# The last 64 rows of a 320-deep product: four half-height products at one place, in the two halves of the rows, in an mLSTM, mixture-of-experts and gated layer kernel

## The chip, the cores and the metric

The kernel runs on one core of a Trainium2 chip. The metric is the device time of one execution in microseconds (us). The kernel before takes 647.97 us (median of three runs, 647.9 to 648.02). TensorE is called PE in the profile and its loading of weights PEld, VectorE is DVE, ScalarE is ACT, GpSimd is POOL, and SyncE (SP) issues the transfers.

## The reference

Three layers follow each other, on 1536 tokens of 320 features.

```python
# 1: mLSTM, 2 batches x 8 heads x 768 steps x 40 features
C = f_stab * C + i_stab * outer(v, k);  n = f_stab * n + i_stab * k
y[t] = sigmoid(o) * (C @ q) / max(|n . q|, 1)
# 2: four experts, D = 320, F = 1024
for e in range(4):
    h = np.maximum(x @ w1[e], 0.0)
    out += p[:, e:e + 1] * (h @ w2[e])
# 3: gated layer, D = 320, F = 1536
return (a * b) @ w_out          # a = x @ w_a, b = x @ w_b
```

All of it is float32. The kernel multiplies in a reduced 32-bit type (`F32R`) and keeps the precision by splitting each operand into a high part and a low part: x = xh + xl, w = wh + wl. A product then is wh·xh + wl·xh + wh·xl; the product of the two low parts is dropped.

## The kernel before, in words

**Blocks.** The weights of layers 2 and 3 are cut into 14 blocks: blocks 0 to 7 for the experts (half an expert, four slices of 128 hidden features each) and blocks 8 to 13 for the gated layer (two slices of 128 hidden features each, with w_a and w_b). Phase one runs layer 1 and, beside it, blocks 0 to 2 on 256 tokens at a time. Phase two runs blocks 3 to 13, each over three chunks `c` of 512 tokens. The two phases are one program on one queue per engine, in the order in which the code records them.

**An item.** An `Item` is one slice `f` of one block on one chunk. Its method `a()` makes the hidden values: one sum (blocks below 8, tile `psa`) or two (blocks 8 and up, `psb` and `psa`) of 128 hidden features by 512 tokens in one of four banks of PSUM that are used in turn; ACT and DVE then make the high part `hh` and the low part `hl` from the sum. Its method `b()` multiplies these by the second weight: 12 products of 320 columns into `psy` (4 groups of 128 tokens, three products each). `Stream.push` calls `a()` of the new item and then `b()` of the item pushed two before it, so TensorE's order is a(f), b(f-2), a(f+1), b(f-1) and so on.

**A sum.** The contraction of 320 is 128 + 128 + 64 rows. `mm_group` makes a sum of eight products of 512 columns and 128 rows each:

```python
(k(wh, 0), x(xh, 0)), (k(wh, 1), x(xh, 1)), (k(wl, 0), x(xh, 0)), (k(wl, 1), x(xh, 1)),
(k(wh, 0), x(xl, 0)), (k(wh, 1), x(xl, 1)), (k(wh, 2), x(xh, 2)), (k(wl, 2), x(xh, 2)),
```

In the third part the 64 rows stand twice: rows 0 to 63 of `xh[c][:, 2]` hold the high part of x and rows 64 to 127 its low part, and the weights stand twice too. So the seventh product gives wh·xh and wh·xl of the last 64 features at once. The eighth gives wl·xh in its upper half; what its lower half adds, low times low, is not needed.

**The split of x.** `split_hi` (ACT) and `split_lo` (DVE) make `xh` and `xl` from the transposed activations in PSUM (`pt_x`, for each of the 12 tiles `n` of 128 tokens): ACT casts all 384 columns to `xh`, DVE makes `xl` (256 columns), and DVE then overwrites rows 64 to 127 of the third part with the low part. This runs 12 times in phase one (`s3b`, and written out for n = 0 and 1) and 12 times around blocks 7 and 8 (`finish_x2`), where the input of layer 3 replaces that of layer 2; there `pt_x2` takes the same four banks of PSUM as the sums, in turn.

**Weights.** The pieces of the blocks are loaded by SP and split by ACT and by DVE or POOL (`piece1`, `piece2`). `Paced` records a stage of them twice an item.

Of the kernel before, what the change touches and what calls it, by code (L numbers as in the profile page):

```python
# [7 lines left out]
F32 = mybir.dt.float32  # L8
F32R = mybir.dt.float32r
BF16 = mybir.dt.bfloat16  # L10
# [3 lines left out]
AF = mybir.ActivationFunctionType  # L14
ALU = mybir.AluOpType
# [3 lines left out]
P = 128  # L19
# [6 lines left out]
NB1, NB2 = 8, 6  # L26
WF1 = 3 * P + DM
WF2 = 6 * P + DM
# [3 lines left out]
NF = 2  # L32
NP = 4
LOENG = {0: "ppvpvpvp", 1: "pppppppp", 2: "pppppppp", 3: "vpvpvpvp", 4: "vpvpvpvp", 5: "vpvpvpvp"}
RB = 3
QB = 3
QENG = ("vector", "vector")
WARM = 10
AHEAD = 2
PACE = ((0, 1.5), (32, 2.4), (62, 2.5))  # L40
NEG = -1.0e30
LOGMIN = -104.0
SQMIN = (1.0625 * 2.0 ** -15) ** 2
# [3 lines left out]
def mlstm_moe_kernel(ctx, tc, gates, qk, qc, kvo, dp, w1b, w2b, ident_d, bdmask_d, rsel_d, exp_d, out):  # L47
    nc = tc.nc
# [3 lines left out]
    wp0 = ctx.enter_context(tc.tile_pool(name="wp0", bufs=3))  # L52
    rawp = ctx.enter_context(tc.tile_pool(name="rawp", bufs=RB))
    xp = ctx.enter_context(tc.tile_pool(name="xp", bufs=1))
# [7 lines left out]

    xh = [xp.tile([P, 3, 512], F32R, name=f"xh{c}") for c in range(3)]
    xl = [xp.tile([P, 2, 512], F32R, name=f"xl{c}") for c in range(3)]
    sums = xp.tile([P, NT * DM], F32, name="acc")
    acc = [sums[:, n * DM:(n + 1) * DM] for n in range(NT)]


    wblk = {}
# [54 lines left out]
    def split_x(ps, c, o):  # L124

        split_hi(ps, c, o)
        split_lo(ps, c, o)
# [3 lines left out]

    def split_lo(ps, c, o):
        nc.vector.tensor_tensor(xl[c][:, :, o:o + P], ps[:, 0:2, :], xh[c][:, 0:2, o:o + P].bitcast(F32), op=ALU.subtract)
        r = xh[c][64:128, 2, o:o + P]
        nc.vector.tensor_tensor(r, ps[64:128, 2, :], r.bitcast(F32), op=ALU.subtract)

# [56 lines left out]
    def mm_group(ps, wh, wl, o0, c, o, n):  # L193
        k = lambda w, t: w[:, o0 + t * P:o0 + (t + 1) * P]
        x = lambda t, i: t[c][:, i, o:o + n]
        prs = [
            (k(wh, 0), x(xh, 0)), (k(wh, 1), x(xh, 1)), (k(wl, 0), x(xh, 0)), (k(wl, 1), x(xh, 1)),
            (k(wh, 0), x(xl, 0)), (k(wh, 1), x(xl, 1)), (k(wh, 2), x(xh, 2)), (k(wl, 2), x(xh, 2)),
        ]
        for i, (l, r) in enumerate(prs):  # L200
            nc.tensor.matmul(ps, l, r, start=(i == 0), stop=(i == len(prs) - 1))  # L201

    class Item:


# [3 lines left out]
        def a(self):  # L209
            blk, f, c, o, n = self.blk, self.f, self.c, self.o, self.n  # L210
            pa, ph = self.pools["a"], self.pools["h"]
            wh, wl = wblk[blk]
            self.hh = ph.tile([P, n], F32R, tag="hh", name="hh")
            self.hl = ph.tile([P, n], F32R, tag="hl", name="hl")
            if blk < NB1:
                ps = pa.tile([P, 512], F32, tag="a", name="psa")[:, :n]
                mm_group(ps, wh, wl, f * WF1, c, o, n)
                nc.scalar.activation(self.hh, ps, AF.Relu)  # L218
                nc.vector.scalar_tensor_tensor(self.hl, ps, 0.0, self.hh.bitcast(F32), op0=ALU.max, op1=ALU.subtract)  # L219
            else:  # L220
                pb = pa.tile([P, 512], F32, tag="a", name="psb")[:, :n]
                mm_group(pb, wh, wl, f * WF2 + 384, c, o, n)
                bs = ph.tile([P, n], F32, tag="bs", name="bs", bufs=2)
                nc.scalar.copy(bs, pb)  # L224
                ps = pa.tile([P, 512], F32, tag="a", name="psa")[:, :n]
                mm_group(ps, wh, wl, f * WF2, c, o, n)
                g = ph.tile([P, n], F32, tag="g", name="g", bufs=2)
                nc.vector.tensor_tensor(g, ps, bs, op=ALU.mult)  # L228
                nc.scalar.copy(self.hh, g)  # L229
                nc.vector.tensor_tensor(self.hl, g, self.hh.bitcast(F32), op=ALU.subtract)  # L230

        def b(self):
            blk, f, fi, nf, n = self.blk, self.f, self.fi, self.nf, self.n
            wh, wl = wblk[blk]
            off = f * WF1 + 384 if blk < NB1 else f * WF2 + 768
            if fi == 0:
                last = (blk, self.c) == (NB1 + NB2 - 1, 2)
                self.pools["bt"] = [self.pools[q].tile([P, DM], F32, tag=q, name="psy") for q in ("aabb" if last else "bbbb")[:n // P]]
            for t in range(n // P):
                ps = self.pools["bt"][t]  # L240
                lh, ll = self.hh[:, t * P:(t + 1) * P], self.hl[:, t * P:(t + 1) * P]
                nc.tensor.matmul(ps, lh, wh[:, off:off + DM], start=(fi == 0), stop=False)  # L242
                nc.tensor.matmul(ps, lh, wl[:, off:off + DM], start=False, stop=False)  # L243
                nc.tensor.matmul(ps, ll, wh[:, off:off + DM], start=False, stop=(fi == nf - 1))  # L244
                if fi == nf - 1:
                    self.done(self.blk, self.c * 4 + self.o // P + t, ps)

    def add_expert(blk, n, ps):
        e = blk // 2
        if blk <= 1:  # L250
            nc.scalar.activation(acc[n], ps, AF.Copy, scale=pg[:, n, 0:1])  # L251
        else:
            nc.vector.scalar_tensor_tensor(acc[n], ps, pg[:, n, e:e + 1], acc[n], op0=ALU.mult, op1=ALU.add)


    stream = Stream(AHEAD)
# [4 lines left out]
    with ExitStack() as c1:  # L261
        cq = ExitStack()
        qp = cq.enter_context(tc.tile_pool(name="qp", bufs=2, side="right"))
        ac = c1.enter_context(tc.tile_pool(name="ac", bufs=1))
# [66 lines left out]
        def gate1(j, eng):  # L331
            mr = a2.tile([G, P + 1], F32, tag="mr", name="mr")
            if j == 0:
                nc.gpsimd.memset(mr[:, 0:1], NEG)
            else:
# [174 lines left out]


        ctx.enter_context(tc.manual_schedule())
        wz = ac.tile([P, 512], BF16, name="wz")
        nc.gpsimd.memset(wz, 0.0)

        def warm_up(n):
# [89 lines left out]
        go(w0[3:4])  # L606
        s2b(1)
        split_lo(td[0]["pv"], 0, 0)
        go(w0[2:4])
        go(w0[4:5])  # L610
        warm_up(4)
        s3a(1)
        split_hi(td[1]["pv"], 0, P)
        split_lo(td[1]["pv"], 0, P)
        warm_up(1)
        go(w0[4:5])
# [18 lines left out]
        for j in range(2, NCH):  # L635
            n0, n1, t0 = 2 * j, 2 * j + 1, NI * (j - 1)
            new = [
                (-6.4, load_kvo, n0), (-6.2, load_o, j, nc.sync), (-2.0, load_kvo, n1),
                (-4.4, load_qk, n0, 0), (-3.4, load_qk, n0, 1), (-2.4, load_qk, n1, 0), (-1.4, load_qk, n1, 1),
                (-4.0, table, AF.Sigmoid), (-3.5, o_gate, j), (-2.5, table, AF.Exp),  # L640
                (-1.5, split_qk, n0, 0), (-0.5, split_qk, n0, 1),
                (0.5, s1a, n0, 0), (1.5, s1a, n0, 1), (1.6, split_qk, n1, 0),
                (2.4, s1b, n0, 0), (2.6, split_qk, n1, 1),
                (3.4, s1b, n0, 1), (3.5, s1a, n1, 0), (3.6, weigh_k, n0),
                (4.2, s2a, n0, 0), (4.5, s2a, n0, 1), (4.6, weigh_k, n1), (4.95, s2b, n0),
# [23 lines left out]
        pools = {"a": ps_a, "b": ps_b, "h": hp}  # L669
# [6 lines left out]
        for k in range(NI * NCH):  # L676
            until(k)
            j, i = k // NI, k % NI
            fi, nf = (i, 8) if i < 8 else (i - 8, 4)
# [10 lines left out]
    pools = {"a": Turns(ps_a2, ps_a), "b": Turns(ps_b2, ps_b), "h": hp2}  # L690
    todo, twice = [], {}

    def finish_x2(n):
        pt = pools["a"].tile([P, 512], F32, tag="a", name="pt_x2")
        pv = pt[:, 0:384].rearrange("p (k t) -> p k t", t=P)
        transpose_x(acc[n], twice[n], pv)
        split_x(pv, n // 4, (n % 4) * P)
# [18 lines left out]
    pieces = [piece1(i, s, slot[i], nc.vector if LOENG.get(i, ())[s:s + 1] == "v" else nc.gpsimd, True) for i in range(4, NB1) for s in range(NP1)]  # L716
    pieces += [piece2(i, s, slot[i]) for i in range(NB1, NB1 + NB2) for s in range(NP2)]
    paced = Paced(pieces, PACE)
    for blk in range(3, NB1 + NB2):
        nf = 4 if blk < NB1 else 2  # L720
        for c in range(3):
            for f in range(nf):
                ready = list(todo)

                def finish(k):
                    for n in ready[:k]:
                        ready.remove(n)
                        todo.remove(n)
                        finish_x2(n)

                def between():
                    paced.step()
                    if blk == NB1:
                        finish(2)

                stream.push(Item(blk, f, f, nf, c, 0, 512, pools, done2), between)
                paced.step()
                finish(2)
    stream.flush()
# [102 lines left out]
```

## Time and profile before

| | |
|---|---|
| median of three runs | 647.97 us |
| the profiled execution, by the clock of the runs | 647.9 us |
| its span in the trace | 646.2 us |
| PE busy | 626.6 us, 97% of the span |
| DVE busy | 419.9 us, 65% |
| ACT busy | 267.2 us, 41% |
| POOL busy | 182.6 us, 28% |
| share of PE in the chain that ended last | 90% |

The span runs from the first to the last instruction of the trace; 1.7 us of the profiled execution lie outside it. Phase one ends at about 221 us. The chain that ended last is followed back from the last instruction, at each step to what released it. A matmul's record is longer than the time that it takes from the next one, since matmuls are pipelined: the distance between starts tells what one costs.

### The profile page before, as it was taken

What the parts mean: (1) busy time and instruction counts of PE and PEld (TensorE: products, weight loads), DVE (VectorE), ACT (ScalarE), POOL (GpSimd) and SP (SyncE); (2) the same over time, 40 slices, a digit from 0 to 9 for tenths busy, and PEclk for the clock granted to TensorE, in tenths of its full rate; (3) what the DMA queues carried; (4) which work ended last, traced back from release to release, by engine and by line L of the source; (5) the groups of instructions that cost most, each with busy time, mean ns of one, the idle gap of its engine ahead of it and who ended that gap; (6) DMA issues with size and microseconds to landing.
All of it is one profiled execution on the core that took longest, in us unless ns stands there. A gap on an engine that the chain in (4) does not pass through costs nothing.

```text
span 646.2 us, 10283 instructions
## 1 busy us (share of the span) xinstructions
PE 626.6 (97%) x3798; PEld 568.6 (88%) x3799; DVE 419.9 (65%) x860; ACT 267.2 (41%) x592; POOL 182.6 (28%) x217
## 2 busy tenths in 40 slices
PE   8887999999999999999999999999999999999997
PEld 6787989999999999999888988888888888888886
DVE  8986858576654244323587888888766776764343
ACT  6774454453614333232343443454544433332221
POOL 4595242525101111233243333322121222220000
PEclk9997999999999999999999999999999999999999
DMA  7873152615201122223122221211111111000003
GB/s 225 241 230 92 40 129 55 166 55 153 71 1 47 44 57 77 59 79 100 45 69 58 65 69 53 71 53 52 36 51 30 43 50 37 18 0 2 1 9 115
DMA packets 27487, 45.99 MB, mean 71 GB/s; under 512 B 3189, under 2 KB 17773, under 8 KB 27437
## 3 DMA queue, kind: packets, MB, share of 16 engines
q1 hardware_dynamic: 27437, 45.33, 25.2%
q8 instruction: 30, 0.49, 0.3%
q14 instruction: 20, 0.16, 0.1%
HBM read 43.35 MB, written 1.97 MB: 70 GB/s over the span
## 4 chain that ended last, share of the span: by engine, by line
PE 90%; DVE 5%; ACT 2%; issue 1%; POOL 1%; DVEq 0%; ACTq 0%; POOLq 0%
PE psa L201 37%; PE psy L242 12%; PE psy L244 11%; PE psy L243 11%; PE psb L201 10%; PE pt_y L435 3%; PE pt_c L417 2%; PE pt_i L441 1%; PE pt_a L407 1%; PE pt_u L485 1%; PE pt_e L389 1%; PE pt_x L140 1%; ACT hh L218 0%; ACT qs_t L301 0%; ACT acc L251 0%
## 5 line engine op out<-in xcount | busy, mean ns | idle before, releaser
L242 PE MATMUL psy<-wh,hh 128*128 128x320 f32 x528 | 166.3, 315 | 1.7 <-ACT acc L251 1.7
L244 PE MATMUL psy<-wh,hl 128*128 128x320 f32 x528 | 163.2, 309 | 0.0
L243 PE MATMUL psy<-wl,hh 128*128 128x320 f32 x528 | 163.1, 309 | 0.0
L201 PE MATMUL psa<-xh,wh 128*128 128x512 f32 (+1 forms) x504 | 149.6, 351 | 1.7 <-DVE hl L219 1.3
L201 PE MATMUL psa<-xh,wl 128*128 128x512 f32 (+1 forms) x504 | 147.1, 346 | 0.0
L219 DVE SCALAR_TENSOR_TENSOR hl<-psa,hh 128x256 fp32r<-128x256 f32 (+1 forms) x132 | 71.7, 543 | 111.7 <-ACT hh L218 111.2
L218 ACT ACTIVATE hh<-psa 128x256 fp32r<-128x256 f32 (+1 forms) x132 | 63.4, 480 | 187.4 <-PE psa L201 185.8
L242 PEld LDWEIGHTS psy<-wh,hh 128*128 128x128 f32 x528 | 99.8, 189 | 8.5 <-ACT acc L251 2.3
L243 PEld LDWEIGHTS psy<-wl,hh 128*128 128x128 f32 x528 | 99.6, 189 | 4.1
L201 PEld LDWEIGHTS psa<-xh,wl 128*128 128x128 f32 x504 | 90.2, 189 | 12.6
L244 PEld LDWEIGHTS psy<-wh,hl 128*128 128x128 f32 x528 | 99.4, 188 | 0.0
L201 PEld LDWEIGHTS psa<-xh,wh 128*128 128x128 f32 x504 | 89.1, 189 | 9.6 <-DVE hl L219 1.5
L201 PE MATMUL psa<-xl,wh 128*128 128x512 f32 (+1 forms) x336 | 88.9, 346 | 0.0
L122 POOL TENSOR_TENSOR wl<-tp,lf 128x272 fp32r<-128x272 f32 x48 | 38.8, 809 | 124.0 <-DVE tp L121 124.0
L201 PEld LDWEIGHTS psa<-xl,wh 128*128 128x128 f32 x336 | 58.4, 189 | 8.2
L228 DVE TENSOR_TENSOR g<-psa,bs 128x512 f32<-128x512 f32 x36 | 24.9, 691 | 50.2 <-PE psa L201 50.2
L119 POOL TENSOR_TENSOR lf<-lf,sq 128x272 f32<-128x272 f32 x48 | 37.5, 782 | 70.3 <-ACT wh L118 39.6
L90 POOL TENSOR_TENSOR wl<-raw,wh 128x352 fp32r<-128x352 f32 x28 | 26.4, 951 | 97.3 <-ACT wh L88 84.3
L229 ACT CAST hh<-g 128x512 fp32r<-128x512 f32 x36 | 22.3, 621 | 72.3 <-DVE g L228 72.3
L409 POOL TENSOR_SCALAR_AFFINE_SELECT w_t<-w_t 128x512 f32<-128x512 f32 x24 | 17.9, 752 | 83.0 <-ACT w_t L408 56.0
L230 DVE TENSOR_TENSOR hl<-g,hh 128x512 fp32r<-128x512 f32 x36 | 24.9, 693 | 24.7 <-ACT hh L229 24.7
L224 ACT COPY bs<-psb 128x512 f32<-128x512 f32 x36 | 21.2, 588 | 44.0 <-PE psb L201 43.9
(118 smaller groups left out, 893.0 us busy)
## 6 DMA issues: line engine op xcount, KB each, us to landing
raw<-in_w2b SPq DMA_DIRECT2D x48, 272.0 KB, 2.7
qk_t<-in_qk SPq DMA_DIRECT2D x16, 480.0 KB, 6.5
raw<-in_w1b SPq DMA_DIRECT2D x40, 176.0 KB, 2.3
acc<-in_w1b SPq DMA_DIRECT2D x24, 176.0 KB, 3.6
kvo_t<-in_kvo SPq DMA_DIRECT2D x10, 364.5 KB, 5.1
og_t<-in_kvo SPq DMA_DIRECT2D x6, 320.0 KB, 6.5
out<-acc SPq DMA_DIRECT2D x12, 160.0 KB, 1.8
qc_t<-in_qc SPq DMA_DIRECT2D x10, 180.0 KB, 3.1
```

The lines of the kernel that those rows point to most:

```text
L90: lo_eng.tensor_tensor(wl[:, cs], raw, wh[:, cs].bitcast(F32), op=ALU.subtract)
L119: nc.gpsimd.tensor_tensor(lf, lf, sq, op=ALU.mult)
L122: nc.gpsimd.tensor_tensor(wl[:, cs], tf, lf, op=ALU.add)
L201: nc.tensor.matmul(ps, l, r, start=(i == 0), stop=(i == len(prs) - 1))
L218: nc.scalar.activation(self.hh, ps, AF.Relu)
L219: nc.vector.scalar_tensor_tensor(self.hl, ps, 0.0, self.hh.bitcast(F32), op0=ALU.max, op1=ALU.subtract)
L228: nc.vector.tensor_tensor(g, ps, bs, op=ALU.mult)
L229: nc.scalar.copy(self.hh, g)
L230: nc.vector.tensor_tensor(self.hl, g, self.hh.bitcast(F32), op=ALU.subtract)
L242: nc.tensor.matmul(ps, lh, wh[:, off:off + DM], start=(fi == 0), stop=False)
L243: nc.tensor.matmul(ps, lh, wl[:, off:off + DM], start=False, stop=False)
L244: nc.tensor.matmul(ps, ll, wh[:, off:off + DM], start=False, stop=(fi == nf - 1))
```

## The change

The sums of phase two are recorded by a new class `Pair`, a kind of `Item`. A sum has seven products as before (`mm_most`, in another order), and the eighth is cut to the 64 rows that are needed (`mm_rest`). Two such 64-row products of two different sums stand one behind the other: one uses rows 0 to 63 of `wl` and of `xh`, the other rows 64 to 127 of `wl` and of a new tile `xq`, a copy of the high part of x that lies in rows 64 to 127. At the last slice of a chunk four of them stand at one place: those that end the third and fourth sum of this chunk, and those that begin the first two sums of the next chunk (the dictionary `begun`). So the third sum waits open until the fourth is there, and its `hh` and `hl` are made one item later. Five chunks, listed in `APART`, make their sums by `mm_group` as before, or end those that the chunk before has begun. The copy `xq` is made in `split_lo`. To make room in SBUF the raw pieces of blocks 3 to 7 have two buffers and not three, and the warm-up tile `wz` moves into `sums`.

```diff
-RB = 3
+RB = 2
+APART = ((NB1 - 1, 1), (NB1 - 1, 2), (NB1, 0), (NB1, 1), (NB1 + NB2 - 1, 2))
+    xq = [xp.tile([P, 512], F32R, name=f"xq{c}") for c in range(3)]
     def split_lo(ps, c, o):
         nc.vector.tensor_tensor(xl[c][:, :, o:o + P], ps[:, 0:2, :], xh[c][:, 0:2, o:o + P].bitcast(F32), op=ALU.subtract)
+        nc.scalar.copy(xq[c][64:128, o:o + P], ps[64:128, 2, :])
         r = xh[c][64:128, 2, o:o + P]
         nc.vector.tensor_tensor(r, ps[64:128, 2, :], r.bitcast(F32), op=ALU.subtract)
+    def mm_most(ps, wh, wl, o0, c, start):
+        k = lambda w, t: w[:, o0 + t * P:o0 + (t + 1) * P]
+        prs = [(wh, 0, xh, 0), (wh, 1, xh, 1), (wh, 2, xh, 2), (wl, 0, xh, 0), (wl, 1, xh, 1), (wh, 0, xl, 0), (wh, 1, xl, 1)]
+        for i, (w, t, x, u) in enumerate(prs):
+            nc.tensor.matmul(ps, k(w, t), x[c][:, u, :], start=start and i == 0, stop=not start and i == len(prs) - 1)
+    def mm_rest(psa, psb, wl, oa, ob, c, start):
+        oa, ob = oa + 2 * P, ob + 2 * P
+        nc.tensor.matmul(psa, wl[0:64, oa:oa + P], xh[c][0:64, 2, :], start=start, stop=not start)
+        nc.tensor.matmul(psb, wl[64:128, ob:ob + P], xq[c][64:128, :], start=start, stop=not start)
+    begun = {}
+    class Pair(Item):
+        def a(self):
...
+            for g in [f] if one else [2 * f, 2 * f + 1]:
+                if (blk, c, g) in begun:
+                    self.q[g] = begun.pop((blk, c, g))
+                    mm_most(self.q[g], wh, wl, at(blk, g), c, False)
+                    continue
+                self.q[g] = new(blk, g)
+                if g < 2 or (blk, c) in APART:
+                    mm_group(self.q[g], wh, wl, at(blk, g), c, 0, 512)
+                    continue
+                mm_most(self.q[g], wh, wl, at(blk, g), c, True)
+                if g == 2:
+                    ready = []
+                    continue
+                ready = [self.prev, self] if one else [self]
+                p2 = self.prev.q[2] if one else self.q[2]
+                mm_rest(p2, self.q[3], wl, at(blk, 2), at(blk, 3), c, False)
+                nb, nc_ = (blk, c + 1) if c < 2 else (blk + 1, 0)
+                for h in range(2):
+                    begun[nb, nc_, h] = new(nb, h)
+                mm_rest(begun[nb, nc_, 0], begun[nb, nc_, 1], wblk[nb][1], at(nb, 0), at(nb, 1), nc_, True)
+            for it in ready:
...
-        wz = ac.tile([P, 512], BF16, name="wz")
+        wz = sums[:, 3520:3776].bitcast(BF16)
-                stream.push(Item(blk, f, f, nf, c, 0, 512, pools, done2), between)
+                item = Pair(blk, f, f, nf, c, 0, 512, pools, done2)
+                item.prev, prev = prev, item
+                stream.push(item, between)
```

The next rows are TensorE's order before, at the end of block 3's chunk 0: the fourth sum, the first products of `b()` of the second item, and then the first sum of chunk 1.

```order
L201 MATMUL psa_2879<-xh0_72,wh3_2426 128x512 x2
L201 MATMUL psa_2879<-xh0_72,wl3_2427 128x512 x2
L201 MATMUL psa_2879<-xl0_75,wh3_2426 128x512 x2
L201 MATMUL psa_2879<-xh0_72,wh3_2426 128x512
L201 MATMUL psa_2879<-xh0_72,wl3_2427 128x512 [waits Pool_49]
L242 MATMUL psy_2857<-wh3_2426,hh_2816 128x320 [waits Activation_49]
```

And the same place now; `psa_2857` is the third sum, `psa_2886` the fourth, and `psa_2896` and `psa_2897` are the first two of chunk 1.

```order
L211 MATMUL psa_2886<-xh0_72,wh3_2439 128x512 x3
L211 MATMUL psa_2886<-xh0_72,wl3_2440 128x512 x2
L211 MATMUL psa_2886<-xl0_75,wh3_2439 128x512 x2
L216 MATMUL psa_2857<-xh0_72,wl3_2440 128x512 [waits Pool_49]
L217 MATMUL psa_2886<-xq0_78,wl3_2440 128x512 [waits Pool_49]
L216 MATMUL psa_2896<-xh1_73,wl3_2440 128x512
L217 MATMUL psa_2897<-xq1_79,wl3_2440 128x512
L258 MATMUL psy_2866<-wh3_2439,hh_2839 128x320 [waits Activation_49]
```

Four products of 64 rows (L216 and L217) stand where one of 128 rows stood, and three sums have one product fewer elsewhere. The changed program has 56 products from `xq`, so 56 such pairs, at 28 places (13 in blocks 3 to 7, 15 in blocks 8 to 13).

ACT's order before, at n = 0 and 1 in the first 20 us of the program:

```order
L130 CAST xh0_72<-pt_x_289 128x3x128 [waits PE_49]
L88 CAST wh0_137<-acc_78 128x352 [waits DMAHW5_49]
L88 CAST wh0_137<-acc_78 128x352 [waits DMAHW7_49]
L496 COPY x_t_300<-x_t_300 128x64 [waits DVE_49]
L130 CAST xh0_72<-pt_x_313 128x3x128 [waits PE_49]
```

And now:

```order
L132 CAST xh0_72<-pt_x_291 128x3x128 [waits PE_49]
L90 CAST wh0_139<-acc_81 128x352 [waits DMAHW5_49]
L136 CAST xq0_78<-pt_x_291 64x128 [waits DVE_49]
L90 CAST wh0_139<-acc_81 128x352 [waits DMAHW7_49]
L561 COPY x_t_302<-x_t_302 128x64
L132 CAST xh0_72<-pt_x_316 128x3x128 [waits PE_49]
```

The copy `xq` (L136) stands between two weight casts, and it waits for DVE: by the program the awaited instruction is `xl` of the same tile of PSUM. DVE's rows at the same place now, where the second subtraction waits for ACT, which it did not before:

```order
L135 TENSOR_TENSOR xl_75<-pt_x,xh_72 128x2x128 [waits Activation_49]
L138 TENSOR_TENSOR xh_72<-pt_x,xh_72 64x128 [waits Activation_49]
L92 TENSOR_TENSOR wl_140<-acc,wh_139 128x352 [waits DMAHW4_49]
L135 TENSOR_TENSOR xl_75<-pt_x,xh_72 128x2x128 [waits Activation_49]
L138 TENSOR_TENSOR xh_72<-pt_x,xh_72 64x128 [waits Activation_49]
```

So the four steps of a split now stand in one line over two engines: cast (ACT), `xl` (DVE), `xq` (ACT), low part of the last 64 rows (DVE). At n = 2 ACT's rows now are these; before, the same rows stood there without L136.

```order
L132 CAST xh0_72<-pt_x_664 128x3x128 [waits PE_49]
L136 CAST xq0_78<-pt_x_664 64x128 [waits DVE_49]
L591 ACT_TABLE_LOAD
L591 ACTIVATE warm_116<-rmask_105 1x1 [waits Activation_49]
L234 ACTIVATE hh_693<-psa_695 128x256 [waits PE_49]
```

A table load and the `hh` of a sum stand behind the copy that waits for DVE.

## Rows read from the trace of the kernel before

**Rows 1.** Busy time by engine, blocks 3 to 7: PE, PEld, DVE, ACT, POOL, clock, DMA

```profile
221.00:438.00 217.00, 217.00 (x1201) 194.50 (x1200) 139.56 (x273) 81.25 (x188) 65.61 (x78) 1.00 0.23 65
```

**Rows 2.** Timeline of PE, an item of block 9: start, duration, instructions

```profile
502.20 0.62 PE L201 MATMUL psb<-xh,wh 128*128 128x512 f32 x2
...
505.92 0.31 PE L242 MATMUL psy<-wh,hh 128*128 128x320 f32 x1
...
507.68 0.62 PE L201 MATMUL psb<-xh,wh 128*128 128x512 f32 x2
```

**Rows 3.** Timeline of PE around the 16-row products of phase one

```profile
130.47 0.27 PE L138 MATMUL pt_x<-ident,x_t 128*128 128x128 f32 x1
130.57 0.27 PE L139 MATMUL pt_x<-ident,x_t 128*128 128x128 f32 x1
...
131.41 0.25 PE L386 MATMUL pt_e<-ident,ex 96*128 96x96 f32 x1
131.59 0.79 PE L389 MATMUL pt_e<-eb,expd 16*120 16x2 f32 x6
```

**Rows 4.** Timeline of PEld, the weight loads at the same place

```profile
131.30 0.14 PEld L386 LDWEIGHTS pt_e<-ident,ex 96*128 96x128 f32 x1
131.59 0.70 PEld L389 LDWEIGHTS pt_e<-eb,expd 16*120 16x120 f32 x6
132.30 0.30 PEld L201 LDWEIGHTS psa<-xh,wh 128*128 128x128 f32 x2
...
133.00 0.19 PEld L201 LDWEIGHTS psa<-xh,wh 128*128 128x128 f32 x1
```

**Rows 5.** Timeline of PEld, the same place without 16-row products

```profile
166.03 0.14 PEld L386 LDWEIGHTS pt_e<-ident,ex 96*128 96x128 f32 x1
166.15 0.30 PEld L201 LDWEIGHTS psa<-xh,wh 128*128 128x128 f32 x2
```

**Rows 6.** The chain that ended last, 13 to 26 us: start, duration, what

```profile
16.88 0.33 DVE xl L133
...
18.57 0.29 DVE xh L135
...
21.32 0.44 DVE hl L219
...
21.80 1.21 PE psa L201 x8
```

**Rows 7.** Timeline of ACT, the splits of n = 0 and 1

```profile
16.14 0.87 ACT L88 CAST wh<-acc 128x352 fp32r<-128x352 f32 x2
16.91 0.25 ACT L496 COPY x_t<-x_t 128x64 f32<-128x64 f32 x1
17.58 0.48 ACT L130 CAST xh<-pt_x 128x384 fp32r<-128x384 f32 x1 [0.42 <-PE pt_x L140]
```

**Rows 8.** Timeline of ACT behind the split of n = 2

```profile
44.54 1.28 ACT L526 ACT_TABLE_LOAD   x1
...
45.95 0.36 ACT L218 ACTIVATE hh<-psa 128x256 fp32r<-128x256 f32 x1
```

**Rows 9.** Timeline of DVE at the split of n = 2

```profile
48.54 0.41 DVE L133 TENSOR_TENSOR xl<-pt_x,xh 128x256 fp32r<-128x256 f32 x1
...
49.30 0.42 DVE L219 SCALAR_TENSOR_TENSOR hl<-psa,hh 128x256 fp32r<-128x256 f32 x1
50.54 0.50 DVE L451 TENSOR_TENSOR y_t<-pt_i,ET 128x328 f32<-128x328 f32 x1 [0.82 <-PE pt_i L441]
```

**Rows 10.** Groups by line, phase two: count, busy us, mean ns, idle before

```profile
L704 ACT COPY twice<-acc 128x128 f32<-128x128 f32 x12 | 3.6, 299 | 7.1 <-DVE acc L253 7.1
```

**Rows 11.** Who waited for whom, PE from 400 us: us, times, longest

```profile
PE psb L201 <- DVE xh L135: 0.6, 1, 0.6
```

**Rows 12.** Timeline of PE, the last product of a third sum of block 6

```profile
373.02 0.39 PE L201 MATMUL psa<-xh,wl 128*128 128x512 f32 x1
```

**Rows 13.** Timeline of DVE, the low part of that sum

```profile
375.23 0.68 DVE L219 SCALAR_TENSOR_TENSOR hl<-psa,hh 128x512 fp32r<-128x512 f32 x1
```

More of the change, by code (lines that the diff above doesn't have):

```diff
@@ L246, in b @@
                     self.done(self.blk, self.c * 4 + self.o // P + t, ps)
+    begun = {}
+    class Pair(Item):
+        def a(self):
+            blk, f, c, one = self.blk, self.f, self.c, self.blk < NB1
+            wh, wl = wblk[blk]
+            pa, ph = self.pools["a"], self.pools["h"]
+            new = lambda b, g: pa.tile([P, 512], F32, tag="a", name="psa" if b < NB1 or g % 2 else "psb")
+            at = lambda b, g: g * WF1 if b < NB1 else g // 2 * WF2 + (g % 2 == 0) * 384
+            self.q, ready = {}, [self]
+            for g in [f] if one else [2 * f, 2 * f + 1]:
[19 more added lines that the diff above has]
+            for it in ready:
+                it.hh = ph.tile([P, 512], F32R, tag="hh", name="hh")
+                it.hl = ph.tile([P, 512], F32R, tag="hl", name="hl")
+                if one:
+                    ps = it.q[it.f]
+                    nc.scalar.activation(it.hh, ps, AF.Relu)
+                    nc.vector.scalar_tensor_tensor(it.hl, ps, 0.0, it.hh.bitcast(F32), op0=ALU.max, op1=ALU.subtract)
+                else:
+                    bs = ph.tile([P, 512], F32, tag="bs", name="bs", bufs=2)
+                    nc.scalar.copy(bs, it.q[2 * f])
+                    g = ph.tile([P, 512], F32, tag="g", name="g", bufs=2)
+                    nc.vector.tensor_tensor(g, it.q[2 * f + 1], bs, op=ALU.mult)
+                    nc.scalar.copy(it.hh, g)
+                    nc.vector.tensor_tensor(it.hl, g, it.hh.bitcast(F32), op=ALU.subtract)
@@ L718, in mlstm_moe_kernel @@
     paced = Paced(pieces, PACE)
+    prev = None
     for blk in range(3, NB1 + NB2):
```

## The prediction

> **What bounds the kernel now.** I read the busy time by stretch first. In blocks 3 to 7 PE is busy all the time, at full clock, while DVE, ACT and POOL have room [rows 1]. So phase two lasts as long as PE's instructions stand apart, and a product that goes saves its distance, whatever other engines do. The timeline of PE gives these distances: an item of block 9 has 16 products of 512 columns from 502.20 to 505.92, so 3.72 / 16 = 0.2325 us each, and then 12 products of 320 columns in 1.76 us [rows 2]. Phase one is different. The chain that ended last runs there over DVE and PE by turns, and it passes through the very step that the change lengthens, the split of x [rows 6]. So two questions decide: what a 64-row place costs PE, and what the copy `xq` costs the chain.
>
> **The products.** Four products of 128 rows become four of 64 rows at each of 28 places. If the two of a pair run beside each other, a place takes two distances and not four: 56 x 0.2325 = 13.0 us are saved. No row shows two products in different halves. The ends are full overlap (13.0 saved) and none (nothing saved); I take full overlap, since the two share no row of the array and no bank, and keep the other end as a rival.
>
> **The switches.** Before and behind each place PE goes from 128-row to 64-row products and back, 56 times in all. The nearest rows are the six 16-row products of phase one. The 96-column transpose in front of them (L386) started at 131.41; transposes of 128 columns stand 0.10 us apart [rows 3], so its 96 columns were through at about 131.49. Yet the load for the first 16-row product started only at 131.59 [rows 4]: 0.10 us in which PE took nothing in, and then the load itself, 0.11 us from its start to the product's (L201's second load starts at 132.30 + 0.30 - 0.19 = 132.41, when its first product does). Where no 16-row products follow, the next load starts 0.12 us behind that of L386 and not 0.29 [rows 5]; in a stream of equal products the load is hidden. The way out looks the same: the six loads end with one that starts at 131.59 + 0.70 - 0.19 = 132.10, its product starts 0.10 later and has two columns, and the next 128-row load starts at 132.30, again 0.10 after it [rows 4]. So a switch costs 0.10 + 0.11 = 0.21 us, and 56 of them 11.8 us. Below, the end is 0, if 64 rows are entered without this pause; I take 0.21, since it was the same in both directions.
>
> The Trainium skill states a rule that speaks against the change here: in TensorEngine Tiling (Array Packing), under Tiling Modes, Key Properties, it says that changing the tiling mode drains the engine. By that rule each place pays twice, which the pause of 0.10 us in rows 3 and 4 agrees with; it gives no time.
>
> **The start of a pair.** The second product of a pair needs its own load, 0.11 us by the rows above. If that starts only with the first product, the pair ends 0.11 us later; if both loads are done together, nothing is added. The second pair follows behind its own halves, so this comes once a place: 0 to 28 x 0.11 = 3.1 us. The ends are close, and I take the middle, 1.5 us.
>
> The Trainium skill (TensorE: Matmul & The Clock Gate, Part 3, The mechanism) puts the starts of such products about 4 ns apart. By that the term of 1.5 us would be about 0.1 us and the sum 1.4 us lower, an estimate from that page; no run here shows it.
>
> PE's part is thus -13.0 + 11.8 + 1.5 = +0.3 us: the switches take back what the pairs save.
>
> **The copy.** `xq` is an ACT copy of 64 x 128 from PSUM; the nearest row is a 128 x 128 copy of 0.30 us [rows 10]. Its place costs more than its length: it waits for `xl` on DVE, the last subtraction waits for it, and on ACT everything recorded behind it waits too.
>
> *At the start.* `xl` of n = 0 ends at 16.88 + 0.33 = 17.21 [rows 6]; a hand-over takes 0.04 (`hl` ends at 21.76, PE starts at 21.80), so `xq` ends at 17.21 + 0.04 + 0.30 = 17.55. The second of the two weight casts, which now stands behind it, began at about 16.14 + 0.87 / 2 = 16.57 [rows 7], so ACT falls 1.0 behind. Next on ACT are the copy at 16.91, which PE's transpose of n = 1 needs, and the cast of n = 1 at 17.58; both move by 1.0. Then the second `xq` puts 0.04 + 0.30 between the subtractions of n = 1. The last of these (18.57) is on the chain, as is `hl` at 21.32, for which PE waits [rows 6]: **+1.3 us**, taken in full since both lie on the chain.
>
> *At n = 2.* The cast is done long before DVE comes to `xl` at 48.54. ACT used that time: a table load at 44.54, and `hh` 1.41 us after it [rows 8]. Now both stand behind `xq`, which ends at 48.54 + 0.41 + 0.04 + 0.30 = 49.29. The table load starts there, `hh` at 50.70, ends at 51.06, and `hl`, which DVE did at 49.30, ends at 51.10 + 0.42 = 51.52. Behind it DVE's `y_t`, 50.54 before [rows 9], starts 1.0 later: **+1.0 us** (the first shift moves all of these alike). I take it in full; the lower end is 0 for both, if a wait that the trace put down to another engine has room. At n = 3 to 11 I count nothing: the later part of phase one is set by PE, which has the products of layer 1 and of two items to do before it needs what waits.
>
> *Around blocks 7 and 8.* Twelve splits come in six pairs. A pair took a cast of 0.48 and twice 0.41 + 0.29 on DVE, about 2.0 us with hand-overs. Now it is one line over two engines, 0.48 + 0.41 + 0.30 for the first and 0.48 + 0.41 + 0.30 + 0.29 for the second with six hand-overs: 2.9 us, 0.9 more. The tile lies in a bank that a sum wants next, and PE waited for such a bank once, 0.6 us [rows 11]. If two of six pairs hold a sum up, it is **+1.8 us**; the ends are 0 (all in the slack) and 5.4 (all six).
>
> **What costs nothing.** The third sum of a chunk gets its `hh` and `hl` an item later. In a late case (block 6) its last product started at 373.02 and `hl` ended at 375.91, 2.9 us after [rows 12, 13]. In the change `b()` wants it after one `b()` of 1.76, seven products (1.63), two of 320 columns (0.29) and its own last product (0.23), 3.9 us: 1.0 us are left. Without that cover each of the 13 places in blocks 3 to 7 would add the excess. Raw buffers: a piece's load now waits for the subtraction two pieces before, not three. PE never waited for weights in that stretch [rows 1], and they are needed a block later. `wz` is no longer used when `sums` needs its place. The chunks in `APART` save nothing and switch nothing; they are not among the 28.
>
> **The sum.** 647.9 (the profiled execution, as the median of the three runs, 647.97; the 1.7 us outside the span stay) + 0.3 + 1.3 + 1.0 + 1.8 = **652.3 us**, 0.7% slower.
>
> **The rivals.**
> - *Cheap switches, faster.* A 64-row place is entered without the pause, or its loads are hidden as in the stream. Then PE's part is -13.0 us at the best, and the time 647.9 - 13.0 + 4.1 = 639.0; with 0.10 a switch (the pause or the load alone) it is 647.9 - 13.0 + 5.6 + 1.5 + 4.1 = 646.1. It decides from (13.0 - 1.5 - 4.1) / 56 = 0.13 us a switch downwards. For it: the only rows are of another height, two columns wide. Against it: the same 0.10 twice.
> - *No overlap.* The two halves run one behind the other, nothing is saved: 647.9 + 11.8 + 4.1 = 663.8. Nothing in the profile speaks for it or against it.
> - *No change to speak of.* The terms of the copy find room (each has 0 as its end) and the switches take back the pairs: 646.7 to 649.2.
> - *A new wait.* `hl` of the third sum comes over 1.0 us too late: with 0.3 us too much at 13 places +3.9, so 656.2. The row above is among the latest, so I count it in the upper part of the forecast.
>
> **How the numbers follow.** The forecast (649.2 to 657.5 with its ends) has 0.46, cheap switches 0.33, no change 0.12, no overlap 0.09. Anything within 0.2%, 1.3 us, can't be told from no change. So faster 0.33, same 0.12, slower 0.46 + 0.09 = 0.55. For eight in ten the range leaves out the lower third of the cheap switches (below 642, about 0.11) and no overlap (above 657.5): 642 to 657.5. The forecast's own range is 649.2 to 657.5.
>
> **What would show it.** Right: at a place, the first 64-row load some 0.10 us after the last 128-row product has streamed, and from the product in front of the four to the first behind them about 1.16 us or a little more (five distances before: 5 x 0.2325); starts of a pair 0.0 to 0.1 apart and pairs one distance apart; PE's first `hl` wait ending near 23.1 and `y_t` of n = 3 near 52.9; longer waits of PE for `xh` between 420 and 462. Wrong: a place that takes 0.7 to 0.9 us (cheap switches), or starts one distance apart within a pair (no overlap), or PE waiting for `hl` at the second item behind each place.

## The result and the profile after

The changed kernel takes 652.57 us (median of four runs, 651.64 to 652.85), the kernel before, run beside it, 648.0 us (four runs, 647.9 to 648.79). The ratio is 1.0065, with an interval of 1.0048 to 1.0083: 0.65% slower. The profiled execution took 652.85 us.

The first lines of the page after, with busy time, share of the span and instructions of each engine, and from its fourth part the share of each engine in the chain that ended last:

```profile
span 651.1 us, 10318 instructions
PE 625.9 (96%) x3799; PEld 554.2 (85%) x3799; DVE 418.3 (64%) x860; ACT 273.8 (42%) x616; POOL 183.3 (28%) x217
PE 80%; DVE 8%; ACT 5%; issue 2%; DMA 1%; POOL 1%; SPq 1%; ACTq 0%; DVEq 0%; POOLq 0%
```

PE is busy almost as long as before (626.6 us), in a span that is 4.9 us longer, and its share of the chain fell from 90% to 80%. So the time did not go into products; PE now waits for DVE and ACT.

**One place.** The timeline of PE and then of PEld, at the end of block 3's chunk 0 (start, duration, instructions). L211 are 128-row products, L216 and L217 the 64-row ones, L258 to L260 those of `b()`:

```profile
234.75 0.63 PE L211 MATMUL psa<-xl,wh 128*128 128x512 f32 x2
235.31 0.50 PE L216 MATMUL psa<-xh,wl 64*128 64x512 f32 x1
235.31 0.50 PE L217 MATMUL psa<-xq,wl 64*128 64x512 f32 x1
235.64 0.39 PE L216 MATMUL psa<-xh,wl 64*128 64x512 f32 x1
235.65 0.39 PE L217 MATMUL psa<-xq,wl 64*128 64x512 f32 x1
235.96 0.42 PE L258 MATMUL psy<-wh,hh 128*128 128x320 f32 x1
236.22 0.31 PE L259 MATMUL psy<-wl,hh 128*128 128x320 f32 x1
```

```profile
234.52 0.42 PEld L211 LDWEIGHTS psa<-xl,wh 128*128 128x128 f32 x2
235.30 0.18 PEld L216 LDWEIGHTS psa<-xh,wl 64*128 64x128 f32 x1 [0.36 <-issue]
235.31 0.18 PEld L217 LDWEIGHTS psa<-xq,wl 64*128 64x128 f32 x1
235.41 0.19 PEld L216 LDWEIGHTS psa<-xh,wl 64*128 64x128 f32 x1
235.41 0.19 PEld L217 LDWEIGHTS psa<-xq,wl 64*128 64x128 f32 x1
235.96 0.19 PEld L258 LDWEIGHTS psy<-wh,hh 128*128 128x128 f32 x1 [0.36 <-issue]
236.07 0.19 PEld L259 LDWEIGHTS psy<-wl,hh 128*128 128x128 f32 x1
```

The two products of a pair start together, and so do their loads: the overlap is full, and a pair has no offset. PEld, which in a stream loads ahead, stands idle for 0.36 us on the way in and on the way out; a load that nothing hides is part of its product's record, so 235.31 is the start of load and product alike. The last product of 128 rows started at 234.75 + 0.63 - 0.40 = 234.98 (a single one lasts 0.40). From there to the second product behind the place, 236.22, it is 1.24 us. Before, the same stretch took five distances of 512 columns and one of 320, 5 x 0.2325 + 0.15 = 1.31 [rows 2]. A place gains 0.07 us.

**The start and n = 2.** ACT's timeline after, first at n = 0 and 1, then at n = 2:

```profile
17.22 0.26 ACT L136 CAST xq<-pt_x 64x128 fp32r<-64x128 f32 x1 [0.61 <-DVE xl L135]
17.51 0.48 ACT L90 CAST wh<-acc 128x352 fp32r<-128x352 f32 x1
17.90 0.24 ACT L561 COPY x_t<-x_t 128x64 f32<-128x64 f32 x1
18.56 0.48 ACT L132 CAST xh<-pt_x 128x384 fp32r<-128x384 f32 x1 [0.42 <-PE pt_x L143]
...
45.28 0.47 ACT L132 CAST xh<-pt_x 128x384 fp32r<-128x384 f32 x1
50.07 0.26 ACT L136 CAST xq<-pt_x 64x128 fp32r<-64x128 f32 x1 [4.31 <-DVE xl L135]
50.34 1.28 ACT L591 ACT_TABLE_LOAD   x1
51.64 0.20 ACT L591 ACTIVATE warm<-rmask 1x1 f32<-1x1 f32 x1
51.87 0.38 ACT L234 ACTIVATE hh<-psa 128x256 fp32r<-128x256 f32 x1
```

PE at the start, and DVE at n = 2:

```profile
23.31 0.51 PE L204 MATMUL psa<-xh,wh 128*128 128x256 f32 x2 [1.58 <-DVE hl L235]
```

```profile
49.62 0.41 DVE L135 TENSOR_TENSOR xl<-pt_x,xh 128x256 fp32r<-128x256 f32 x1
50.36 0.29 DVE L138 TENSOR_TENSOR xh<-pt_x,xh 64x128 fp32r<-64x128 f32 x1 [0.33 <-ACT xq L136]
52.28 0.42 DVE L235 SCALAR_TENSOR_TENSOR hl<-psa,hh 128x256 fp32r<-128x256 f32 x1 [1.63 <-ACT hh L234]
52.62 0.49 DVE L516 TENSOR_TENSOR y_t<-pt_i,ET 128x328 f32<-128x328 f32 x1
```

The copy itself takes 0.26 us. At the start the weight cast behind it begins at 17.51 and not near 16.57, the copy `x_t` and the cast of n = 1 follow 1.0 us later than before [rows 7], and PE, which was released at 21.80 [rows 6], starts at 23.31, 1.5 us later. At n = 2 ACT stands 4.31 us in front of the copy until DVE has done `xl`; then come the table load (44.54 before [rows 8]), `hh` and `hl`, and `y_t` starts at 52.62 and not at 50.54 [rows 9]: 2.1 us in all.

**Blocks 7 and 8.** Who waited for whom, PE from 404 to 480 us: us in all, times, longest:

```profile
PE psb L204 <- DVE xh L138: 2.1, 2, 1.4
PE psy L258 <- DVE acc L318: 1.2, 1, 1.2
PE psa L204 <- DVE xh L138: 0.3, 1, 0.3
```

Before, there was one such wait, of 0.6 us [rows 11]. Now they make 3.6 us: 3.0 more. Three are for the low part of the last 64 rows, the last instruction of the lengthened line; the fourth is for DVE's additions to `acc`, which come later because DVE waits inside the splits (0.33 us for each copy).

**The balance.** The starts of the same products of `b()` in both traces (`psy`, counted from the first of the program) show where the time went:

| product | before, us | after - before |
|---|---|---|
| 1st | 22.8 | +1.52 |
| 73rd | 70.7 | +3.17 |
| 433rd (phase two begins) | 228.4 | +3.47 |
| 1009th (block 7) | 402.6 | +2.88 |
| 1225th (blocks 7 and 8 done) | 489.5 | +6.37 |
| 1584th, the last | 642.2 | +5.00 |

Between n = 2 (+2.1) and the 73rd product lies 1.1 us more that no step of the change explains; it is told at the end, since a stretch at half clock lasts longer in this execution.

### The profile page after: what moved, and what is told of

It reads as the page before. It is cut to its first block, busy times and chain, and to the rows that moved or that the text cites. A ratio compares the mean times of both kernels' runs of the same rounds, so it can differ in the third digit from the quotient of the medians.

```text
span 651.1 us, 10318 instructions
## 1 busy us (share of the span) xinstructions
PE 625.9 (96%) x3799; PEld 554.2 (85%) x3799; DVE 418.3 (64%) x860; ACT 273.8 (42%) x616; POOL 183.3 (28%) x217
## 4 chain that ended last, share of the span: by engine, by line
PE 80%; DVE 8%; ACT 5%; issue 2%; DMA 1%; POOL 1%; SPq 1%; ACTq 0%; DVEq 0%; POOLq 0%
PE psa L211 20%; PE psy L258 11%; PE psa L204 11%; PE psy L260 10%; PE psy L259 10%; PE psb L211 7%; PE pt_y L500 2%; PE psb L216 1%; PE psa L216 1%; PE pt_c L482 1%; DVE acc L318 1%; PE pt_i L506 1%; DMA og_t<-in_kvo 1%; ACT hh L303 1%; PE psb L204 1%
## 5 line engine op out<-in xcount | busy, mean ns | idle before, releaser
L258 PE MATMUL psy<-wh,hh 128*128 128x320 f32 x528 | 169.5, 321 | 3.8 <-ACT acc L316 1.9
L260 PE MATMUL psy<-wh,hl 128*128 128x320 f32 x528 | 163.2, 309 | 0.0
L258 PEld LDWEIGHTS psy<-wh,hh 128*128 128x128 f32 x528 | 99.9, 189 | 19.6 <-issue 13.4
L260 PEld LDWEIGHTS psy<-wh,hl 128*128 128x128 f32 x528 | 99.4, 188 | 0.0
L304 DVE SCALAR_TENSOR_TENSOR hl<-psa,hh 128x512 fp32r<-128x512 f32 x60 | 40.2, 688 | 74.7 <-ACT hh L303 74.2
L211 PE MATMUL psa<-xh,wh 128*128 128x512 f32 x246 | 70.1, 393 | 0.0
L204 PE MATMUL psa<-xh,wh 128*128 128x256 f32 (+1 forms) x258 | 66.2, 311 | 2.3 <-DVE hl L235 1.6
L204 PE MATMUL psa<-xh,wl 128*128 128x256 f32 (+1 forms) x258 | 64.2, 304 | 0.0
L303 ACT ACTIVATE hh<-psa 128x512 fp32r<-128x512 f32 x60 | 34.4, 596 | 68.3 <-PE psa L211 41.0
L235 DVE SCALAR_TENSOR_TENSOR hl<-psa,hh 128x256 fp32r<-128x256 f32 x72 | 30.2, 419 | 41.9 <-ACT hh L234 41.6
L234 ACT ACTIVATE hh<-psa 128x256 fp32r<-128x256 f32 x72 | 27.4, 381 | 70.0 <-PE psa L204 68.4
L211 PE MATMUL psa<-xh,wl 128*128 128x512 f32 x164 | 51.1, 393 | 0.0
L211 PE MATMUL psa<-xl,wh 128*128 128x512 f32 x164 | 50.8, 391 | 0.0
L211 PEld LDWEIGHTS psa<-xh,wh 128*128 128x128 f32 x246 | 44.0, 188 | 6.0
L204 PEld LDWEIGHTS psa<-xh,wl 128*128 128x128 f32 x258 | 44.8, 194 | 1.9
```

Source lines behind the costliest of these rows:

```text
L211: nc.tensor.matmul(ps, k(w, t), x[c][:, u, :], start=start and i == 0, stop=not start and i == len(prs) - 1)
L303: nc.scalar.activation(it.hh, ps, AF.Relu)
L304: nc.vector.scalar_tensor_tensor(it.hl, ps, 0.0, it.hh.bitcast(F32), op0=ALU.max, op1=ALU.subtract)
```

## The experiments

**The copy without the places.** Every chunk in `APART`; the copy, the two raw buffers and the class stay, no product of 64 rows is left.

```diff
-APART = ((NB1 - 1, 1), (NB1 - 1, 2), (NB1, 0), (NB1, 1), (NB1 + NB2 - 1, 2))
+APART = tuple((b, c) for b in range(3, NB1 + NB2) for c in range(3))
```

> The copy xq stays where it is, every chunk is listed in APART, so no 64-row product is left and all sums have eight products of 128 rows. Theory (the copy costs, the places give a little back): the changed kernel's trace shows about 3.7 us lost by the end of phase one and 3.5 us around blocks 7 and 8, so 648.0 + 7 = 654 to 655 us, slower than the changed kernel by the 2 us that 28 places give. Rival (the places and their switches cost the time, the copy is hidden): 648.0 us. Second rival (half and half): 650 us.

Measured: 653.74 us (four runs, 652.75 to 653.92), 1.0087 (1.0074 to 1.0101) of the kernel before. The copy alone costs more than the whole change, so the places, with the order that they need, give back 1.2 us by the medians; phase two of the two traces gives 0.6 (told in the account below). The time was a little below the 654 to 655 us expected.

**The places without the ACT copy.** `xq` comes by SP transfers from the rows 0 to 63 of `xh`, three in front of phase two and three as the chunks of `finish_x2` are done.

```diff
     def split_lo(ps, c, o):
-        nc.scalar.copy(xq[c][64:128, o:o + P], ps[64:128, 2, :])
...
+    def copy_hi(c):
+        nc.sync.dma_start(xq[c][64:128, :].bitcast(F32), xh[c][0:64, 2, :].bitcast(F32))
...
+    for c in range(3):
+        copy_hi(c)
...
+        if n % 4 == 3:
+            copy_hi(n // 4)
```

> The 28 places stay, the copy leaves ACT: three transfers between the phases and three around blocks 7 and 8 put the high part of x from rows 0 to 63 of xh into rows 64 to 127 of xq. Theory: no line over two engines is left, only the places act, 28 x 0.07 us = 2.0 us gained: 646.0 us, between 645.5 and 646.8. Rival (the places cost): 652 us, no better than the changed kernel. Second rival (the transfers hold up SP's queue and with it the weights of blocks 11 to 13): 647 to 650 us.

Measured: 646.86 us (eleven runs, 645.58 to 647.37), 0.9982 (0.9973 to 0.9991). That is the upper edge of what was expected, and 1.2 us below the kernel before; in this are the order and the two raw buffers beside the places. The second rival falls: from the first product of `b()` of block 11 to the last it takes 86.8 us here and in the changed kernel, whose copies are on ACT. PE's waits between 404 and 480 us are back at what they were before:

```profile
PE psb L203 <- DVE xh L137: 0.6, 1, 0.6
```

**The order alone.** The products stand where the change puts them, but all of 128 rows, and there is no `xq`.

```diff
...
-        nc.tensor.matmul(psa, wl[0:64, oa:oa + P], xh[c][0:64, 2, :], start=start, stop=not start)
-        nc.tensor.matmul(psb, wl[64:128, ob:ob + P], xq[c][64:128, :], start=start, stop=not start)
+        nc.tensor.matmul(psa, wl[:, oa:oa + P], xh[c][:, 2, :], start=start, stop=not start)
+        nc.tensor.matmul(psb, wl[:, ob:ob + P], xh[c][:, 2, :], start=start, stop=not start)
```

> The order of the changed kernel without its two other parts: at each place stand four products of 128 rows, as the eighth products were before, and there is no xq and no copy of it. What is saved and what is switched both go. Theory (moving the products and keeping the third sum open costs nothing): 648.0 us, within 0.3. Rival (hh and hl of the third sum come too late, or a bank is free too late): 649.5 us and more, with waits of PE at the second item behind each place.

Measured: 647.67 us (eleven runs, 647.09 to 648.5), 0.9995 (0.9986 to 1.0003). The time tells no cost of holding the third sum open, of the later `hh` and `hl` and of two raw buffers together. The trace tells more: with two raw buffers the products of phase two stand closer (see the last experiment), and the order takes most of that back. Between 221 and 404 us PE has waits that the kernel before and the copy alone don't have:

```profile
PE psy L256 <- DVE acc L316: 0.6, 3, 0.2
```

They are for DVE's additions to `acc`, in front of the first products of `b()` in three chunks. The first sum of such a chunk is one product shorter there, so its `b()` comes sooner behind the products that the additions need.

**The same half.** All four products of a place use rows 0 to 63, and there is no `xq`.

```diff
...
-        nc.tensor.matmul(psb, wl[64:128, ob:ob + P], xq[c][64:128, :], start=start, stop=not start)
+        nc.tensor.matmul(psb, wl[0:64, ob:ob + P], xh[c][0:64, 2, :], start=start, stop=not start)
```

> All four products of a place take rows 0 to 63 of wl and xh, so both of a pair use the same half, and there is no xq and no copy. Theory (only different halves run beside each other): nothing is saved, the switches stay, 28 x 0.39 = 11 us lost: 659 us, and up to 668 if a load into the half that is in use can't be hidden either (three loads of 0.11 us a place). Rival (64-row products are as cheap wherever they stand): 646 us.

Measured: 659.84 us (four runs, 659.71 to 660.11), 1.0184 (1.0168 to 1.02). The timeline of PE at the same place:

```profile
233.07 0.50 PE L214 MATMUL psa<-xh,wl 64*128 64x512 f32 x1
233.41 0.39 PE L215 MATMUL psa<-xh,wl 64*128 64x512 f32 x1
233.63 0.40 PE L214 MATMUL psa<-xh,wl 64*128 64x512 f32 x1
233.87 0.39 PE L215 MATMUL psa<-xh,wl 64*128 64x512 f32 x1
234.19 0.42 PE L256 MATMUL psy<-wh,hh 128*128 128x320 f32 x1
```

Now the starts are a full distance apart: half the rows alone save nothing, the overlap comes from the two halves. And since against the kernel with the order alone only the switches are new, their price is seen bare: (659.84 - 647.67) / 56 = 0.22 us each, and 0.21 by phase two of the traces alone.

**The copy in one phase at a time.** ACT copies in phase one and transfers fetch the input of layer 3; then the other way round.

```diff
...
-        nc.scalar.copy(xq[c][64:128, o:o + P], ps[64:128, 2, :])
+        if first[0]:
+            nc.scalar.copy(xq[c][64:128, o:o + P], ps[64:128, 2, :])
```

(`if not first[0]` in the second kernel; `first[0]` is set to False where phase two begins, and `copy_hi` is called for the other part.)

> The copy on ACT stays in phase one alone (n = 0 to 11 once); around blocks 7 and 8 three transfers make xq instead. The 28 places stay. Theory (the line over two engines costs some 2 us in phase one and 3.5 us around blocks 7 and 8): 2.0 to 2.3 us above the kernel with all copies by transfers (646.9), so 649 us, with PE's wait for hl ending about 1.1 us later at the start and y_t of n = 3 about 2.0 us later. Rival (all of the loss is at the end of phase one or later): 647 us.

> The reverse: transfers between the phases, the copy on ACT only in the twelve splits around blocks 7 and 8. Theory: 3.5 us above the kernel with all copies by transfers, so 650.4 us; the two halves then add up to the changed kernel (646.9 + 2.2 + 3.5 = 652.6). My forecast had 1.8 us for this part, so 648.7 us, if the changed kernel's 3.5 us come from something else.

Measured: 649.47 us (ten runs, 648.55 to 649.73; 1.0019, 1.001 to 1.0029) and 649.88 us (six runs, 649.16 to 650.64; 1.0027, 1.0016 to 1.0039). Against 646.86 with no ACT copy the first costs 2.6 us and the second 3.0. They add up: 646.86 + 2.6 + 3.0 = 652.5, and the change has 652.57. The second kernel has the four waits of PE that are shown above, to the tenth. By the traces alone the first costs 2.2 us up to the start of phase two and the second 3.4 in phase two; the differences of 0.4 lie within what the stretch at half clock (below) changes.

**The wait or the work.** The same copy on ACT, but recorded directly behind the cast, so that it no longer waits for `xl`.

```diff
     def split_hi(ps, c, o):
         nc.scalar.copy(xh[c][:, :, o:o + P], ps)
+        nc.scalar.copy(xq[c][64:128, o:o + P], ps[64:128, 2, :])
...
     def split_lo(ps, c, o):
         nc.vector.tensor_tensor(xl[c][:, :, o:o + P], ps[:, 0:2, :], xh[c][:, 0:2, o:o + P].bitcast(F32), op=ALU.subtract)
-        nc.scalar.copy(xq[c][64:128, o:o + P], ps[64:128, 2, :])
```

> The copy stays on ACT and reads PSUM, but stands right behind the cast of the same tile and so in front of xl: ACT waits for nothing new, DVE waits for one more ACT instruction. Theory (the waits between the engines cost, not the 0.26 us of the copy): most of the 5.7 us comes back; some 0.3 us a split where the chain passes (n = 1, n = 2, six pairs) stay, so 647.5 to 648.7 us. Rival (ACT's time is what costs): 652 us, like the changed kernel.

Measured: 646.15 us (eight runs, 645.92 to 647.45), 0.9972 (0.9962 to 0.9982), the fastest kernel of the study, and below the 647.5 to 648.7 expected. ACT at n = 2 and PE's waits between 404 and 480 us:

```profile
44.39 0.47 ACT L132 CAST xh<-pt_x 128x384 fp32r<-128x384 f32 x1
44.89 0.26 ACT L133 CAST xq<-pt_x 64x128 fp32r<-64x128 f32 x1
45.17 1.28 ACT L591 ACT_TABLE_LOAD   x1
```

```profile
PE psb L204 <- DVE xh L138: 0.8, 2, 0.6
```

The copy is as long as before, 0.26 us, and does the same work twelve times in each phase. With the wait in front of it, it cost 5.6 us; without, nothing that the time can tell from transfers that take ACT's place altogether (PE waits once more, for 0.2 us). How much of the 5.6 us is ACT's wait for `xl` and how much DVE's for the copy was not separated.

**Twice the switches.** As with the transfers, but the pair that begins the next sums stands in front of the fourth sum's seven products, so that a place becomes two.

```diff
+                if g == 3:
+                    nb, nc_ = (blk, c + 1) if c < 2 else (blk + 1, 0)
+                    for h in range(2):
+                        begun[nb, nc_, h] = new(nb, h)
+                    mm_rest(begun[nb, nc_, 0], begun[nb, nc_, 1], wblk[nb][1], at(nb, 0), at(nb, 1), nc_, True)
                 mm_most(self.q[g], wh, wl, at(blk, g), c, True)
...
-                nb, nc_ = (blk, c + 1) if c < 2 else (blk + 1, 0)
-                for h in range(2):
-                    begun[nb, nc_, h] = new(nb, h)
-                mm_rest(begun[nb, nc_, 0], begun[nb, nc_, 1], wblk[nb][1], at(nb, 0), at(nb, 1), nc_, True)
...
```

> As the kernel with the copies by transfers, but the four products of a place stand at two: the pair that begins the next chunk's sums goes in front of the fourth sum's seven products, the pair that ends the third and fourth sum stays behind them. Twice the switches, the same products saved. Theory (a switch costs 0.197 us, from 4 x 0.2325 less the 0.072 that a place gave, over two switches): 56 more of them, 11.0 us: 646.9 + 11.0 = 658 us. Rival (the pause is there but hidden or paid once a chunk): 647 us.

Measured: 658.12 us (four runs, 656.72 to 658.37), 1.0148 (1.0133 to 1.0164). Against 646.86 that is 11.3 us for 56 more switches, 0.20 us each. With the price known, a pair that stands alone saves one distance, 0.23, and pays 0.40, so it loses 0.17. Two pairs at one place save 0.465 for the same 0.40: that is what makes it pay at all, and only just.

**Where the tiles lie.** In every kernel with two raw buffers the products of 512 columns stand at other distances than before, in the order of before too. Two kernels, of one run each: the kernel before with two raw buffers and nothing else, and the same with an unused tile (`pad`) that puts the tiles of x back.

```diff
-RB = 3
+RB = 2
...
+    pad = xp.tile([P, 352], F32, name="pad")
```

> The kernel before with two raw buffers and nothing else of the change, so the tiles of x lie 1408 bytes lower in SBUF. Theory (the distance between two 512-column products depends on where the operands lie): the mean distance by block goes over to that of all kernels with two buffers, blocks 4 to 6 from 232.2 to about 231 ns, 9 and 10 from 232.3 to about 228.5, 12 from 229.3 to about 232, 7 from 230.4 to about 232; the span about 0.5 us shorter, 645.5 to 646.0. Rival (the changed order of products does it): the distances stay as in the kernel before.

> As the kernel with two raw buffers, but an unused tile of 1408 bytes a row in front of the tiles of x puts these back where they were. Theory (place of the operands): distances as in the kernel before, blocks 9 and 10 at 232.3 ns, 12 at 229.3. Rival (the number of raw buffers itself, by what it does to DVE, POOL and the transfers): as with two buffers and no such tile, blocks 9 and 10 about 228.5, 12 about 232.

The first products of the item of rows 2 and of the next item, with two raw buffers, and with the unused tile as well:

```profile
502.95 0.63 PE L201 MATMUL psb<-xh,wh 128*128 128x512 f32 x2
...
508.36 0.63 PE L201 MATMUL psb<-xh,wh 128*128 128x512 f32 x2
```

```profile
503.47 0.62 PE L202 MATMUL psb<-xh,wh 128*128 128x512 f32 x2
...
508.95 0.62 PE L202 MATMUL psb<-xh,wh 128*128 128x512 f32 x2
```

An item takes 5.41 us with two buffers and 5.48 with the unused tile, and took 5.48 before (502.20 to 507.68 [rows 2]). Over whole blocks the mean distance goes from 232.3 to 228.3 ns in blocks 9 and 10 and from 229.3 to 232.2 in block 12, and with the unused tile it is 232.3 and 229.3 again. So the place of the operands in SBUF does it. From the first product of `b()` in phase two to the last, two raw buffers alone gain 1.3 us, and with the unused tile nothing. The expected gain in the time was not seen: the two took 648.05 and 649.16 us beside 648.06, since both begin phase two 1.3 to 1.5 us later, most of it by the stretch at half clock (below).

## Why the prediction was right, and where only its sum was

The forecast was 652.3 and the time 652.57. Its mechanism holds: the switches take back nearly all that the pairs save, and the copy makes the kernel slower. That the sum comes so close is luck. Two terms were off by about 1.5 us each, in opposite directions, and three that it had at nothing or not at all (the order, the place of the operands, the stretch at half clock) nearly cancel as well.

- **The products, right.** Full overlap: the pairs start together, and with all in one half the time is 659.84.
- **The switches, right.** 0.21 us were forecast. The same pause of 0.10 and the load of 0.11 stand in the rows of the place, in both directions, although its products are of another height and length than those of rows 3 and 4. The same-half kernel gives 0.21 to 0.22, twice the switches 0.20.
- **The start of a pair, mis-sized.** The 1.5 us taken between 0 and 3.1 are about 0: both loads start within 0.01 us of each other, and so do both products. The Trainium skill (TensorE: Matmul & The Clock Gate, Part 3, The mechanism) has this as about 4 ns. The trace agrees with it, at 0 to 0.01 us.
- So **PE's part** was not +0.3 us: the places gain. The time from the first product of `b()` in phase two to the last, one trace each, tells the parts apart:

| kernel | us | step |
|---|---|---|
| before | 413.9 | |
| two raw buffers alone | 412.6 | -1.3, the place of the operands |
| the order alone (two raw buffers too) | 413.4 | +0.8, the order |
| the places, copies by transfers | 411.9 | -1.5, the places |
| the change | 415.4 | +3.5, the copy around blocks 7 and 8 |

- The places gain 0.05 us each and not the 0.07 reckoned above with the distances of the kernel before. With the order alone the same stretch takes 1.29 us on average over the 28 places, since the products stand closer there, and in the change it takes 1.23.
- **The copy at the start and at n = 2, right.** 2.3 us were forecast; `y_t` starts 2.1 us later, and phase one's copy alone costs 2.6 by the times. The mechanism is the one forecast, down to the table load behind the copy.
- **The copy around blocks 7 and 8, mis-sized.** 1.8 us were taken between 0 and 5.4; it is 3.0 by the times and 3.5 by the traces. Three waits for a split are there, one of them 1.4 us long, and less the 0.6 us of before they make just the 1.8. What the prediction didn't see is the fourth, 1.2 us for the additions to `acc`: a wait inside a split also delays what stands behind it on DVE.
- **What costs nothing, right for the wait that it looked at.** No wait of PE for the third sum's `hl` shows between 221 and 404 us. But the order costs 0.8 us in blocks 3 to 7, 0.6 of it in the three waits for additions to `acc`, and the two raw buffers gain 1.3 by where they put the operands. Neither was in the forecast.

The rivals: no overlap falls with the overlap, cheap switches with 0.20 to 0.22 us measured, no change with the 5.6 us that the copy costs, and the new wait since PE waits for no `hl` there. By the times, the kernel with transfers is 1.2 us below the kernel before and the copy adds 5.6: 647.9 - 1.2 + 5.6 = 652.3 again.

## What to carry to other kernels

Before a copy is put into a line of steps, look at what it waits for and what stands behind it on its queue, not at its length alone: 24 copies of 0.26 us cost 5.6 us where they waited for another engine, and nothing that the time tells where they stood right behind the cast. Products of half the rows pay only in two halves and in runs: each entry and each exit cost 0.2 us here, nearly a product of 512 columns, so put as many pairs as possible at one place. A total that comes out right proves no term of it; kernels with one part alone showed that two were wrong. Nor does a time that stays the same prove that nothing happened: in the order alone a gain and a loss cancel.

## What the runs showed that was not expected

**The distance of products depends on where their operands lie in SBUF.** The same product of 512 columns takes 228 to 234 ns by block; a shift of the tiles of x by 1408 bytes a row changes it by up to 4 ns. In phase two this gained the change 1.3 us, as two raw buffers alone show. Which places are good was not tried.

**A stretch at half clock varies by about 1 us.** Busy time by stretch behind the gap of phase one: PE, PEld, DVE, ACT, POOL, granted clock, DMA share, GB/s, first before, then after, then the kernel before with two raw buffers:

```profile
55.00:60.00 5.00, 1.08 (x8) 0.62 (x6) 4.49 (x6) 2.25 (x5) 4.92 (x5) 0.78 0.09 28
60.00:65.00 5.00, 4.91 (x22) 4.89 (x23) 1.14 (x4) 1.63 (x4) 1.90 (x2) 0.54 0.72 173
65.00:70.00 5.00, 5.00 (x40) 4.91 (x39) 4.02 (x9) 2.52 (x6) 1.34 (x2) 1.00 0.00 0
```

```profile
60.00:65.00 5.00, 2.85 (x13) 2.84 (x14) 2.67 (x3) 0.57 (x3) 3.95 (x3) 0.50 0.34 90
65.00:70.00 5.00, 5.00 (x25) 4.90 (x25) 2.46 (x5) 2.36 (x5) 0.05 (x1) 0.58 0.30 83
```

```profile
55.00:60.00 5.00, 1.38 (x10) 0.93 (x8) 4.51 (x5) 2.55 (x6) 4.92 (x5) 1.00 0.10 34
60.00:65.00 5.00, 4.59 (x20) 4.58 (x21) 1.36 (x4) 1.44 (x4) 2.21 (x2) 0.51 0.67 173
65.00:70.00 5.00, 5.00 (x34) 4.91 (x32) 3.24 (x7) 1.49 (x6) 0.72 (x1) 0.80 0.00 0
```

Between 55 and 60 us PE is mostly idle. Before, the clock fell to its lower level (1.2 GHz) within that time and was back at the full level (2.4 GHz) by about 65 us; with two raw buffers, in nearly the same program, it fell later, beside PE's work, and came back later too. The 73rd `psy` product then starts 1.2 us later, and the changed kernel's profile has 1.1 us of the same kind. The two raw buffers don't settle it: the order alone has them too, and its 73rd product starts only 0.2 us later. Runs of one kernel differ too: the kernel before took 646.97 to 648.86 us in 21 runs. What sets the moment of the fall is open, so a term of 1 us of phase one in a single trace proves nothing here. The times above are medians of four to eleven runs (one run each for where the tiles lie), and the parts of phase two are read behind this stretch.
